# A planned kernel on one core: products of ones, split halves, one more vt load, joined additions, and a new order of all steps

## The chip, the cores and the metric
One core of a Trainium2 chip. The metric is device microseconds of one execution, as the median of three. Times inside an execution come from one profiled execution and count from its first instruction.

## The reference
q, k and v are float32 of shape (4, 5056, 256), normal values times 0.1. Per batch:
```python
qn = q / (norm(q, axis=1) + 1e-6);  kn = k / (norm(k, axis=1) + 1e-6)
s = kn.T @ qn / tau                      # 256 x 256
a = softmax(s, axis=-1)
x = v @ a                                # 5056 x 256
```
Then a soft mixture of 8 experts with 4 slots each over all 20224 rows x: `logits = x @ phi` (32 columns); softmax over the rows gives the slots' inputs `d.T @ x`; each expert computes `relu(in @ w1) @ w2` (256 to 1024 to 256); softmax over the 32 columns weights the slots' outputs into the result (20224 x 256).

## The kernel before
Five engines and one DMA queue (SP's) work through one list of steps. A program of `at(...)` calls puts some thousand steps into `plan`; ORDER, a list of numbers worked out beforehand, says in which order they are called (lines 1037 to 1039). Each engine takes its own steps in that order, and so does SP's queue. A step whose inputs are not there holds up all that stand behind it on its engine.

- SBUF has 22 big buffers of 1 MB. HOME says which buffer a tile takes; the tile waits until all readers of the buffer's tile before it are done.
- q and k come in 40 units u (4 batches, 10 units each; batches share units 9 and 29, called MIX): tile raw{u}, up to four row blocks j of 128 rows. `load_qk` (line 141) loads unit 0 in two parts, and all others in one.
- `score(u, j, split)` (line 237) adds a row block into k.T @ q. Plain, it multiplies the float32 tile (two products, each of which the trace shows as two matmuls). For the halves (u, k) in SPLIT, `cast` (ScalarE) and `low` (VectorE, line 209) first make a high and a low part in a tile hl{u}_{k}, and score makes three products of each of the two column halves: six matmuls for a row block.
- `square` (ScalarE) and `add` (VectorE, lines 232 to 235) sum the squares of the columns, for the norms. Before, the additions of units 11 to 38 come as two instructions of 1024 columns, those of units 1 to 9 as one of 2048.
- v comes in 20 tiles p of eight row blocks. x = v @ a is never formed: v's transpose (tile x{p}) is multiplied with the small matrix M = a @ phi (`logits`, line 393). Each half m of that transpose is loaded from a copy in memory (`load_vt`, line 156) if (p, m) is in LT; otherwise TensorE turns it (`turn`, line 373: four transposes for each half h) and ScalarE evicts it (`turned`).
- `gather` (line 495) sums the slots' inputs; the steps join_ and last_ put them together; `up`, `relu`, `flip_h`, `back_h`, `down` (lines 671 to 717) are the experts. `down(r, h, f)` makes the column half h and needs w2 tiles of that half. `o_copy`, `o_fold`, `o_back` finish a half; then `out_mul` (line 740) and `out_evict` make the result of a row tile, `store` writes it. Ten stores of batch 0 go by column halves, the first half's before the second half's downs are done.
- `c_max` to `c_flip` are the softmax over the columns, on VectorE and ScalarE.
- `wake` (line 784) multiplies ones with ones on TensorE, at the very start.

Of the kernel before, what the change touches and what calls it, by code (L numbers as in the profile page):

```python
# [20 lines left out]
WAKE = 9  # L21
PITCH = 128
NU = B * UB
NRAW = 5
MIX = (UB - 1, 3 * UB - 1)
SPLIT = {(u, 0) for u in range(1, NU) if u not in (1, 2, 3, 17, 20, 27, 31)} | {(u, 1) for u in (2, 5, 14, 24, 26, 27, 31, 33, 35, 37, 39)}
LT = {(p, 0) for p in (0, 2, 3, 4, 5, 6, 7, 8, 9, 11, 12, 13, 15, 18, 19)} | {(p, 1) for p in (0, 3, 6, 9, 12, 15)}
GR = {b: (3, 2) for b in range(B)}
HOME = {
    "raw0": 0, "raw1": 1, "raw2": 2, "raw3": 3, "raw4": 4, "sq0": 5, "sq1": 6, "sq2": 8, "hl2_1": 7, "sq3": 18,  # L30
    "hl4_0": 19, "sq4": 20, "v1": 8, "raw5": 9, "raw6": 10, "raw9": 11, "raw8": 12, "raw7": 13, "v4": 7, "hl5_0":
    21, "sq5": 6, "hl6_0": 1, "x1": 20, "hl5_1": 0, "hl9_0": 2, "sq6": 3, "sq9": 7, "sq10": 6, "hl8_0": 8, "hl7_0":
    18, "raw13": 17, "sq8": 20, "sq7": 4, "raw12": 0, "raw10": 16, "x0": 18, "raw16": 19, "raw17": 14, "hl13_0": 4,
    "sq13": 10, "hl10_0": 7, "hl12_0": 17, "x4": 0, "sq12": 16, "raw14": 13, "v2": 14, "raw18": 12, "hl14_1": 14,
    "hl14_0": 4, "sq17": 3, "hl16_0": 18, "sq14": 10, "hl18_0": 11, "v5": 19, "raw19": 15, "raw11": 21, "raw15": 1,
    "v7": 13, "sq16": 16, "sq19": 20, "hl19_0": 9, "hl15_0": 13, "hl11_0": 16, "sq15": 0, "raw20": 2, "raw21": 15,
    "x2": 21, "raw24": 19, "sq18": 1, "sq11": 3, "hl24_1": 6, "sq20": 1, "sq21": 12, "hl21_0": 10, "hl24_0": 3,
    "sq24": 15, "raw23": 5, "raw25": 4, "v0": 2, "raw22": 9, "raw28": 11, "x5": 8, "raw29": 17, "hl23_0": 10,
    "sq23": 20, "hl25_0": 21, "sq22": 12, "sq25": 3, "hl28_0": 10, "hl22_0": 18, "raw26": 16, "x3": 5, "raw27": 20,
    "raw31": 11, "sq28": 9, "sq29": 6, "sq30": 14, "hl29_0": 18, "hl26_0": 5, "hl27_1": 16, "sq26": 10, "x7": 6,  # L40
    "sq27": 21, "raw30": 15, "v3": 9, "v8": 21, "raw32": 3, "hl26_1": 15, "hl31_1": 18, "sq31": 1, "hl32_0": 20,
    "sq32": 5, "hl30_0": 2, "x6": 10, "v11": 15, "raw33": 12, "raw34": 0, "raw37": 1, "raw38": 17, "hl33_1": 2,
    "sq33": 15, "hl34_0": 10, "hl33_0": 8, "x8": 11, "sq37": 2, "sq34": 16, "hl37_1": 9, "raw39": 4, "v6": 12,
    "v10": 7, "x9": 9, "x12": 1, "x11": 13, "raw36": 5, "raw35": 3, "hl38_0": 6, "sq39": 20, "hl37_0": 18, "sq38":
    12, "hl39_1": 12, "sq36": 19, "x10": 10, "sq35": 8, "v13": 2, "v17": 20, "v9": 0, "v14": 16, "v19": 11,
    "hl35_1": 21, "hl35_0": 10, "hl36_0": 11, "x13": 6, "hl39_0": 19, "x14": 0, "x15": 8, "x18": 13, "v18": 5,
    "v16": 17, "v12": 18, "w1_0": 15, "x19": 12, "x17": 10, "x16": 3, "nat0": 1, "v15": 19, "w1_1": 4, "w1_7": 7,
    "w1_3": 6, "w1_4": 14, "w1_6": 9, "w1_2": 21, "w1_5": 18, "nat3": 12, "w2_1_0": 3, "w2_0_0": 0, "w2_2_0": 8,
    "w2_3_0": 10, "w2_1_1": 16, "w2_0_1": 2, "w2_2_1": 1, "w2_3_1": 13, "nat2": 19, "hs0": 17, "hT0": 20, "hs1": 5,
    "hT1": 11, "o0_1": 15, "o0_2": 4, "o0_0": 21, "o0_4": 6, "o0_3": 17, "o3_3": 14, "o3_1": 9, "o2_1": 18, "nat1":  # L50
    7, "o2_2": 5, "o3_2": 0, "o2_0": 8, "o3_4": 3, "o2_4": 2, "o3_0": 10, "o1_2": 16, "o1_3": 20, "o1_4": 1, "o1_0":
    11, "o1_1": 13, "o2_3": 12,
# [3 lines left out]
    1, 7, 14, 18, 0, 2, 3, 5, 4, 9, 12, 11, 20, 10, 21, 28, 6, 13, 38, 29, 634, 22, 113, 135, 49, 76, 8, 15, 23, 30,  # L56
    34, 39, 43, 50, 47, 77, 26, 27, 36, 37, 25, 17, 16, 19, 24, 31, 35, 44, 40, 51, 48, 78, 54, 81, 68, 59, 63, 72,
    174, 55, 69, 60, 83, 175, 64, 73, 531, 532, 32, 57, 56, 33, 46, 42, 45, 53, 52, 75, 84, 74, 65, 66, 79, 80, 71,
    61, 41, 181, 92, 159, 161, 121, 177, 91, 156, 87, 114, 178, 118, 70, 176, 182, 122, 533, 85, 103, 67, 93, 123,
    86, 145, 58, 601, 163, 155, 173, 88, 115, 119, 534, 82, 535, 111, 117, 62, 89, 116, 143, 162, 112, 160, 144,  # L60
    154, 108, 104, 164, 146, 124, 128, 120, 109, 536, 110, 538, 165, 147, 158, 157, 105, 129, 125, 537, 132, 530,
    150, 98, 140, 136, 171, 153, 172, 185, 186, 131, 107, 90, 539, 130, 391, 387, 149, 148, 126, 127, 167, 166, 198,
    187, 102, 197, 106, 133, 134, 179, 152, 540, 151, 137, 141, 180, 543, 183, 607, 602, 600, 189, 219, 599, 231,
    190, 94, 168, 392, 541, 388, 544, 194, 191, 142, 95, 170, 546, 169, 99, 100, 551, 552, 193, 545, 389, 192, 139,
    542, 397, 138, 97, 96, 390, 228, 547, 398, 184, 548, 385, 399, 101, 188, 386, 549, 220, 210, 400, 608, 614, 199,
    603, 598, 553, 437, 440, 393, 272, 217, 218, 271, 282, 196, 195, 554, 211, 221, 212, 213, 223, 222, 395, 208,
    555, 224, 438, 200, 214, 441, 550, 394, 204, 264, 229, 556, 230, 215, 225, 216, 558, 439, 201, 265, 557, 236,
    396, 239, 226, 443, 559, 266, 407, 207, 240, 227, 267, 203, 206, 205, 445, 237, 238, 442, 560, 446, 606, 605,
    241, 609, 209, 444, 232, 268, 447, 278, 250, 233, 269, 448, 449, 280, 454, 563, 281, 270, 251, 273, 263, 253,
    333, 615, 604, 202, 235, 401, 234, 450, 453, 463, 467, 455, 274, 561, 564, 258, 242, 285, 402, 289, 451, 408,  # L70
    275, 259, 252, 286, 260, 571, 452, 572, 284, 612, 610, 613, 616, 283, 290, 262, 261, 300, 276, 288, 277, 287,
    403, 299, 573, 246, 456, 292, 316, 468, 247, 457, 574, 566, 243, 458, 293, 405, 249, 562, 565, 309, 245, 244,
    248, 575, 279, 296, 459, 567, 460, 254, 485, 461, 297, 298, 317, 568, 306, 569, 404, 320, 472, 481, 464, 469,
    323, 617, 311, 620, 621, 576, 462, 255, 482, 466, 312, 324, 406, 465, 302, 411, 318, 257, 483, 409, 256, 473,
    310, 295, 319, 294, 307, 471, 322, 308, 313, 475, 484, 578, 325, 321, 303, 476, 470, 328, 365, 362, 410, 412,
    474, 570, 477, 354, 486, 332, 331, 304, 327, 417, 326, 305, 619, 301, 611, 622, 291, 618, 329, 363, 487, 479,
    355, 577, 418, 382, 493, 488, 491, 501, 505, 579, 315, 372, 357, 314, 423, 421, 358, 489, 345, 349, 369, 424,
    422, 342, 364, 383, 330, 490, 580, 492, 359, 495, 384, 366, 370, 583, 346, 350, 496, 353, 373, 413, 419, 360,
    356, 361, 348, 368, 581, 494, 506, 420, 414, 497, 584, 582, 415, 585, 352, 347, 416, 587, 627, 629, 626, 637,
    623, 625, 633, 624, 755, 638, 640, 371, 499, 343, 351, 586, 588, 427, 431, 367, 589, 498, 378, 374, 478, 428,  # L80
    502, 510, 519, 507, 435, 344, 590, 375, 504, 591, 520, 379, 334, 338, 503, 436, 432, 592, 511, 335, 593, 639,
    628, 631, 750, 753, 632, 594, 433, 521, 429, 509, 513, 522, 595, 430, 512, 508, 434, 381, 336, 337, 524, 656,
    650, 673, 523, 597, 339, 525, 480, 500, 765, 766, 514, 651, 657, 596, 380, 340, 654, 425, 341, 377, 376, 655,
    515, 426, 636, 648, 652, 635, 517, 767, 667, 670, 649, 653, 768, 668, 671, 526, 529, 666, 674, 669, 672, 528,
    675, 677, 681, 769, 678, 642, 646, 679, 676, 643, 647, 680, 644, 527, 516, 645, 683, 702, 692, 664, 662, 686,
    689, 770, 518, 771, 709, 832, 684, 688, 694, 835, 691, 712, 665, 663, 703, 658, 660, 704, 705, 751, 630, 641,
    752, 756, 749, 757, 754, 763, 761, 759, 758, 659, 661, 687, 682, 690, 714, 716, 695, 760, 833, 834, 685, 706,
    698, 717, 831, 697, 715, 713, 693, 718, 764, 762, 699, 707, 721, 722, 719, 701, 708, 724, 720, 723, 700, 696,
    726, 728, 731, 725, 733, 710, 786, 732, 727, 729, 734, 730, 740, 741, 735, 736, 711, 737, 742, 738, 743, 745,
# [14 lines left out]
def colnorm_attention_soft_moe(  # L104
# [59 lines left out]
    def load_few():  # L164
        sp.dma_start(few_sb, few)

    load_qk(0, ((0, 1), (1, 4)))
    for u in range(1, NRAW):
        load_qk(u)

# [621 lines left out]
    def at(key, f, *a):  # L792
        plan.append((key, len(plan), f, a))

    at(-2, wake, WAKE)
    FV = 13
# [299 lines left out]
```

## Time and profile before

| | us |
|---|---|
| median of 3 runs | 277.02 (276.91 to 278.49) |
| profiled execution | 277.06 |
| its span, first to last instruction | 275.3 |
| TensorE busy | 254.6 (92%) |
| VectorE busy | 236.8 (86%) |
| ScalarE busy | 195.5 (71%) |
| moved by DMA | 111.44 MB, 405 GB/s over the span |

The span is shorter than the time by 1.76 us, which lie outside the recorded instructions. Matmuls overlap, so TensorE's busy time is the time in which at least one was under way. The DMA share is the mean busy share of the 16 DMA engines; it can come out slightly over 1. "Landing" of a DMA is the time from its issue by SP to its completion.

### The profile page before, as it was taken

Reading aid. Unit: us, or ns where it says so; the run is one execution under the profiler, and the core shown is the slowest. Engines: PE = TensorE matmul, PEld = TensorE weight load, DVE = VectorE, ACT = ScalarE, POOL = GpSimd, SP = SyncE. Lnnn points to the kernel's source line nnn. Section 1 sums busy time; section 2 is a strip of 40 time slices with the busy share of each in tenths; the row PEclk is TensorE's granted clock in tenths of the full one; section 3 lists DMA queues with packets and bytes.
Section 4 is the critical chain, followed back from the end, with each engine's and each line's share of the span. In section 5 each row is a group of like instructions: output and inputs, shape, how many; then the busy total and the mean of one; then the engine's idle time right before and its main releaser. Section 6 shows DMA issues by size and latency. Waiting matters only on the chain.

```text
span 275.3 us, 6127 instructions
## 1 busy us (share of the span) xinstructions
PE 254.6 (92%) x2494; PEld 212.6 (77%) x2494; DVE 236.8 (86%) x349; ACT 195.5 (71%) x285; POOL 7.5 (3%) x12
## 2 busy tenths in 40 slices
PE   8999999999999999999999999999999988678730
PEld 8889998999998896997898978866555878457520
DVE  1599999999999999999999997887989879988630
ACT  3898989798899689899998783886416247353430
POOL 1000002000002000020000001000000000000000
PEclk9999999999999999999999999999999999855755
DMA  7999999999999999999999999999999789999995
GB/s 283 432 424 410 422 426 415 420 417 419 419 417 420 412 422 421 416 415 417 412 419 418 416 417 419 417 416 420 421 415 420 300 332 388 418 418 412 420 421 246
DMA packets 17883, 111.44 MB, mean 405 GB/s; under 512 B 2112, under 2 KB 2112, under 8 KB 6592
## 3 DMA queue, kind: packets, MB, share of 16 engines
q1 hardware_dynamic: 17856, 111.06, 98.0%
q8 instruction: 19, 0.31, 0.4%
q14 instruction: 8, 0.07, 0.1%
HBM read 90.08 MB, written 20.97 MB: 403 GB/s over the span
## 4 chain that ended last, share of the span: by engine, by line
PE 87%; DVE 6%; ACT 3%; issue 1%; DVEq 0%; ACTq 0%
PE S L255 46%; PE op_None L750 8%; PE L L403 7%; PE G L503 7%; PE vTp L376 6%; PE op L750 3%; PE O L711 2%; DVE o L774 2%; ACT o L772 2%; PE wake L787 2%; PE Mp L347 1%; PE nn L266 1%; DVE nat L630 1%; DVE cm L627 1%; PE sp L549 1%; PE gt L525 1%
## 5 line engine op out<-in xcount | busy, mean ns | idle before, releaser
L235 DVE TENSOR_TENSOR sq<-sq,sq 128x1024 f32<-128x1024 f32 (+1 forms) x61 | 81.3, 1356 | 8.4 <-ACT sq L220 8.0
L220 ACT ACTIVATE sq<-raw 128x2048 f32<-128x2048 f32 (+1 forms) x40 | 74.7, 1889 | 6.5 <-DMA raw<-in_qk_dram 4.8
L255 PE MATMUL S<-hl 128*128 128x256 f32 x516 | 71.5, 291 | 0.0
L255 PE MATMUL S<-raw 128*128 128x256 f32 (+1 forms) x296 | 66.9, 384 | 0.0
L255 PEld LDWEIGHTS S<-hl 128*128 128x128 f32 x516 | 65.2, 191 | 1.0
L255 PEld LDWEIGHTS S<-raw 128*128 128x128 f32 (+1 forms) x296 | 53.7, 192 | 8.1 <-issue 1.5
L209 DVE TENSOR_TENSOR hl<-raw,hl 128x1024 fp32r<-128x1024 f32 x43 | 51.6, 1219 | 0.7 <-ACT hl L204 0.7
L204 ACT CAST hl<-raw 128x1024 fp32r<-128x1024 f32 x43 | 44.0, 1048 | 6.1 <-PE S L255 2.5
L750 PE MATMUL op_None<-so,lg 32*128 32x256 f32 x240 | 26.4, 525 | 6.0 <-ACT o L772 4.1
L772 ACT COPY o<-op_None 128x512 f32<-128x512 f32 x30 | 15.8, 594 | 18.2 <-PE op_None L750 17.9
L750 PEld LDWEIGHTS op_None<-so,lg 32*128 32x128 f32 x240 | 19.6, 251 | 11.6 <-ACT o L772 6.3
L381 ACT COPY x<-vTp 128x512 f32<-128x512 f32 x38 | 21.5, 593 | 9.3 <-PE vTp L376 8.8
L774 DVE COPY o<-op_None 128x512 f32<-128x512 f32 x30 | 19.0, 678 | 8.0 <-PE op_None L750 8.0
L376 PE MATMUL vTp<-ident,v 128*128 128x128 f32 x152 | 21.6, 276 | 0.0
L403 PE MATMUL L<-x,M 128*32 128x256 f32 (+1 forms) x320 | 20.3, 379 | 0.0
L376 PEld LDWEIGHTS vTp<-ident,v 128*128 128x128 f32 x152 | 17.3, 143 | 2.8 <-issue 2.5
L503 PE MATMUL G<-v,dn 128*32 128x256 f32 x320 | 19.1, 381 | 0.0
L503 PEld LDWEIGHTS G<-v,dn 128*32 128x32 f32 x320 | 10.8, 110 | 5.9 <-issue 0.7
L403 PEld LDWEIGHTS L<-x,M 128*32 128x32 f32 x320 | 9.8, 109 | 6.2 <-issue 0.8
L750 PE MATMUL op<-so,lg 32*128 32x128 f32 x160 | 9.6, 315 | 2.0 <-ACT o L772 1.4
L750 PEld LDWEIGHTS op<-so,lg 32*128 32x128 f32 x160 | 7.7, 197 | 4.4 <-ACT o L772 2.7
L772 ACT COPY o<-op 128x256 f32<-128x256 f32 x20 | 6.4, 378 | 6.3 <-PE op L750 6.3
(112 smaller groups left out, 233.0 us busy)
## 6 DMA issues: line engine op xcount, KB each, us to landing
raw<-in_qk_dram SPq DMA_DIRECT2D x37, 1024.0 KB, 12.5
v<-in_v_dram SPq DMA_DIRECT2D x20, 1024.0 KB, 11.1
w<-in_moe_w_dram SPq DMA_DIRECT2D x16, 1024.0 KB, 17.5
out_dram<-o SPq DMA_DIRECT2D x15, 1024.0 KB, 7.5
x<-in_vt_dram SPq DMA_DIRECT2D x17, 512.0 KB, 10.2
out_dram<-o SPq DMA_DIRECT2D x10, 512.0 KB, 3.7
raw<-in_qk_dram SPq DMA_DIRECT2D x3, 768.0 KB, 10.0
x<-in_vt_dram SPq DMA_DIRECT2D x4, 480.0 KB, 11.9
```

What stands on the lines that cost most here:

```text
L204: act.copy(hl[:, :, 0::2, :], raws[u][:, 2 * k : 2 * k + 2])
L209: dve.tensor_tensor(hl[:, :, 1::2, :], raws[u][:, 2 * k : 2 * k + 2], hl[:, :, 0::2, :].bitcast(F32), op=ALU.subtract)
L220: act.activation(sq_tile(u)[:, :n], raws[u][:, :n], AF.Square)
L235: dve.tensor_tensor(a[:, lo:hi], a[:, lo:hi], s[:, lo:hi], op=ALU.add)
L255: pe.matmul(sm, w, x, start=first[bb], stop=False, skip_group_check=True)
L376: pe.transpose(tp[:, P * jj : P * jj + P], vs[p][:, 4 * h + jj, P * m : P * m + P], ident)
L381: act.copy(x[:, h * UT : h * UT + UT], tps[p, h, m])
L403: pe.matmul(L[S * g : S * g + S, :n, :], M[:, m, :], x[:, :n, S * g : S * g + S], start=m == 0, stop=m == 1,)
L503: pe.matmul(gp[S * g : S * g + S, :C], dn[:, x, j, :], vt[:, j, :], start=x == 0 and j < G, stop=x == n - 1 and j >= G,)
L750: pe.matmul(ops[b, p, hf, g][:, h, :], cT[b][S * g : S * g + S, 4 * i : 4 * i + 4, :].rearrange("s j t -> s (j t)"), so[S * g : S * g + S] ...
L772: act.copy(dst, src)
L774: dve.tensor_copy(dst, src)
```

## The change
- WAKE: six products of ones instead of nine.
- Unit 0 is loaded as row blocks 0 and 1, then 2 and 3 (512 KB each), instead of 0, then 1 to 3.
- SPLIT: 40 halves instead of 43. (5,0), (5,1), (7,0), (13,0), (19,0), (27,1), (32,0), (37,0), (39,0) become plain; (8,1), (11,1), (13,1), (23,1), (27,0), (34,1) become split.
- LT: (14, 0) is added. One vt load of 512 KB more, two turns (and evictions) fewer: 957 steps in place of 992, with the additions.
- `add`: one instruction of 2048 columns for units 11 to 38 too (26 pairs); unit 39 keeps two.
- HOME and ORDER are new throughout.

```diff
-WAKE = 9
+WAKE = 6
...
-SPLIT = {(u, 0) for u in range(1, NU) if u not in (1, 2, 3, 17, 20, 27, 31)} | {(u, 1) for u in (2, 5, 14, 24, 26, 27, 31, 33, 35, 37, 39)}
-LT = {(p, 0) for p in (0, 2, 3, 4, 5, 6, 7, 8, 9, 11, 12, 13, 15, 18, 19)} | {(p, 1) for p in (0, 3, 6, 9, 12, 15)}
+SPLIT = {(u, 0) for u in range(1, NU) if u not in (1, 2, 3, 5, 7, 13, 17, 19, 20, 31, 32, 37, 39)} | {(u, 1) for u in (2, 8, 11, 13, 14, 23, 24, 26, 31, 33, 34, 35, 37, 39)}
+LT = {(p, 0) for p in (0, 2, 3, 4, 5, 6, 7, 8, 9, 11, 12, 13, 14, 15, 18, 19)} | {(p, 1) for p in (0, 3, 6, 9, 12, 15)}
...
+    1, "x10": 13, "v11": 4, "raw36": 7, "raw35": 9, "v13": 15, "x12": 6, "v17": 1, "v9": 19, "v14": 11, "hl38_0":
+    20, "sq38": 16, "sq36": 10, "x11": 21, "hl35_1": 18, "sq35": 0, "hl35_0": 16, "hl36_0": 3, "x13": 5, "hl39_1":
+    12, "x14": 20, "v12": 10, "v16": 0, "w2_0_0": 7, "x15": 2, "v18": 19, "w1_6": 13, "w1_7": 8, "v19": 9, "x17":
...
-    load_qk(0, ((0, 1), (1, 4)))
+    load_qk(0, ((0, 2), (2, 4)))
...
         if i:
-            if u > 9:
-                at(u + (0.55 if u < NU - 1 else 0.05), add, u, 0, 2)
-                at(u + (0.72 if u < NU - 1 else 0.06), add, u, 2, 4)
+            if u == NU - 1:
+                at(u + 0.05, add, u, 0, 2)
+                at(u + 0.06, add, u, 2, 4)
             else:
                 at(u + 0.60, add, u, 0, 4)
```
ORDER, read as steps, where the text below needs it (f(u, ...) as in the code; the last argument of score is split):
```
TensorE, start, new: wake; score (0,0) (0,2) (0,1) (0,3) (1,1) (1,0) (1,2) (2,1) (2,0) (1,3) (3,2) (3,0) (3,3) (3,1) (4,2) (5,0) (5,3) (4,3) (6,2) (6,3), all plain
SP, new:            ... load_v(9) load_v(14) load_vt(12,1) load_vt(14,0) load_vt(11,0) load_vt(13,0) load_v(12) load_v(16) load_w2(0,0) ...
TensorE, new:       ... turn(13,1,1) turn(10,0,1) score(38,0,1) att_phi(2) gather(8) gather(9) logits(10) turn(14,1,1) ...
TensorE, before:    ... att_phi(2) turn(13,1,1) turn(14,0,1) score(38,0,1) logits(10) gather(8) gather(9) ...
TensorE, before:    ... down(1,0,*) down(0,1,0) o_fold(0) down(0,1,6) out_mul down(0,1,2) out_mul down(0,1,4) out_mul out_mul down(1,1,*) out_mul o_fold(1) ...
TensorE, new:       ... down(1,0,*) o_fold(0) down(0,1,0) out_mul down(0,1,4) out_mul down(0,1,2) out_mul down(0,1,6) out_mul down(1,1,*) out_mul o_fold(1) ...
SP, last loads:     before w2 (0,1) (1,1) (3,1) (2,1); new w2 (0,1) (1,1) (2,1) (3,1)
ScalarE:            before relu(0,0) relu(0,1) c_exp(3) relu(1,1) c_exp(2) back_h(0,1) relu(1,0); new relu(0,1) relu(0,0) c_exp(3) c_exp(2) relu(1,1) relu(1,0) back_h(0,1)
```

## Rows read from the trace of the kernel before
**Rows 1.** The page: span, and the granted TensorE clock in 40 slices.
```profile
span 275.3 us, 6127 instructions
PEclk9999999999999999999999999999999999855755
```
**Rows 2.** Stages: start:end, length; busy us (xinstructions) of each engine, clock, DMA share, GB/s.
```profile
0.00:158.00 158.00, 156.96 (x1212) 141.46 (x1212) 146.75 (x175) 138.59 (x152) 6.47 (x11) 1.00 1.00 413
12.00:165.00 153.00, 153.00 (x1260) 136.69 (x1258) 150.52 (x177) 137.30 (x158) 5.77 (x5) 1.00 1.02 418
165.00:200.00 35.00, 35.00 (x434) 25.43 (x433) 28.59 (x78) 21.64 (x61) 1.01 (x1) 1.00 1.02 417
200.00:217.40 17.40, 16.93 (x265) 10.69 (x261) 16.45 (x24) 6.49 (x10) 0.00 (x0) 1.00 0.99 411
217.40:229.00 11.60, 10.71 (x253) 8.88 (x253) 8.72 (x22) 5.56 (x19) 0.00 (x0) 1.00 0.74 295
229.00:272.40 43.40, 28.03 (x255) 20.91 (x251) 29.56 (x44) 17.77 (x35) 0.00 (x0) 0.65 1.01 415
```
**Rows 3.** The chain of waits in order of time: start us, us, what, instructions.
```profile
73.33 1.43 PE S L255 x12
79.29 1.73 PE S L255 x8
148.53 0.87 PE vTp L376 x8
158.08 0.81 PE Mp L347 x8
159.80 0.71 PE S L255 x6
216.86 0.57 PE O L711 x16
222.41 1.89 PE O L711 x64
224.29 0.73 PE op L750 x16
```
**Rows 4.** Groups by form, VectorE and ScalarE: busy us, mean ns of one, idle before.
```profile
L235 DVE TENSOR_TENSOR sq<-sq,sq 128x1024 f32<-128x1024 f32 x53 | 63.0, 1215 | 0.4 <-ACT sq L220 0.2
L209 DVE TENSOR_TENSOR hl<-raw,hl 128x1024 fp32r<-128x1024 f32 x43 | 51.6, 1219 | 0.7 <-ACT hl L204 0.7
L204 ACT CAST hl<-raw 128x1024 fp32r<-128x1024 f32 x43 | 44.0, 1048 | 6.1 <-PE S L255 2.5 <-DMA raw<-in_qk_dram 2.5 <-DVE sq L235 0.6
L235 DVE TENSOR_TENSOR sq<-sq,sq 128x2048 f32<-128x2048 f32 x8 | 18.3, 2289 | 8.0 <-ACT sq L220 7.8
```
**Rows 5.** Timeline of the start: start us, us, engine, line, operation, idle before.
```profile
0.73 5.17 SPq L146 DMA_DIRECT2D raw<-in_qk_dram  x10
1.04 4.21 PE L787 MATMUL wake<-ones 128*128 128x128 f32 x18 [1.04 <-DVE half L176]
4.84 11.24 PEld L255 LDWEIGHTS S<-raw 128*128 128x128 f32 x49
5.65 1.91 ACT L220 ACTIVATE sq<-raw 128x2048 f32<-128x2048 f32 x1 [3.43 <-DMA raw<-in_qk_dram]
...
5.05 14.67 PE L255 MATMUL S<-raw 128*128 128x256 f32 x64
```
**Rows 6.** DMA from 0 to 16 us in 40 bins; an issue, its us to landing.
```profile
GB/s 0 0 0 0 128 195 364 353 384 399 445 446 481 369 389 492 430 328 492 471 348 471 451 389 430 451 430 348 512 451 328 471 471 369 430 492 389 389 430 492
raw<-in_qk_dram SPq DMA_DIRECT2D x1, 256.0 KB, 2.6
```
**Rows 7.** Timeline of SP's queue: issues of loads, start us, us.
```profile
157.40 1.04 SPq L154 DMA_DIRECT2D v<-in_v_dram  x2
...
195.40 5.29 SPq L666 DMA_DIRECT2D w<-in_moe_w_dram  x3
```
**Rows 8.** Issues and us to landing: the second of those at 157.4, the last w.
```profile
v<-in_v_dram SPq DMA_DIRECT2D x1, 1024.0 KB, 16.0
w<-in_moe_w_dram SPq DMA_DIRECT2D x1, 1024.0 KB, 19.9
```

## What the change will do, predicted before it ran
> **What bounds the kernel now.** The table by stage comes first [rows 2]: from 12 to 165 us TensorE is busy in all of the 153 us and the DMA engines are full (share 1.02, 418 GB/s); so it stays to 200 us. Two resources are at their limit together. From 200 to 217.4 us TensorE still works 16.93 of 17.40 us (the expert stage) and the queue still carries loads. Only from 217.4 to 229 us does the DMA drop, to 295 GB/s: the loads have ended and the outputs are not yet there in number. From 229 to 272.4 us stores run at 415 GB/s, and the kernel ends with them; the clock that TensorE has lost by then [rows 1] costs nothing. So the end is set by (a) when out_mul for the two halves of batch 0 can start and (b) the bytes that are left then. (a) hangs on TensorE's total work and on the landing of the last w2 tiles, which stand at the end of one SP queue: the last three were issued in 5.29 us from 195.4 on, the last of them near 200.4 [rows 7], and took 19.9 us to land [rows 8], so 220.3 us.
>
> How much the DMA can give at all: the dip costs 11.6 us x (1 - 295/418) = 3.4 us. Closing all of it, with 1.26 us of new bytes (below), would bring 2.1 us, 0.8%.
>
> **TensorE's work.** In the chain of waits, in order of time, twelve split products (two tiles) take 1.43 us and eight plain ones (two tiles) 1.73 us [rows 3]. A half unit therefore costs 0.30 us more plain than split. Splits fall from 43 to 40 halves: +0.90 us. Two turns fewer at 0.87/2 us: -0.87 us. Sum +0.03 us, nothing. All else on TensorE is the same set of steps in another order.
>
> **VectorE and ScalarE.** Three casts at 1.05 us (-3.1 us) and two evictions of turns leave ScalarE. Three subtractions at 1.22 us leave VectorE, and 26 pairs of additions become one: 2 x 1.215 - 2.289 = 0.14 us each, 3.7 us [rows 4]. These 7.4 us lie beside a full TensorE [rows 2], and after 200 us VectorE's steps are the same ones, so I cost them at zero; if TensorE were waiting for VectorE, the relief would be worth up to that much. It isn't: TensorE shows no idle there. GpSimd's few steps keep their places among the norms and lie beside the same work. The Trainium skill (VectorE: DVE Perf Modes, section "The TRN2 errata") says that every SBUF-source instruction pays a fixed extra, about 150 cycles of 0.96 GHz; by it, as an estimate, a pair joined saves 0.16 us and all 26 save 4.1 us. The rows say nearly the same, and the sum is the same by both, since none of it is on the path.
>
> **The start.** Nine products of ones are 18 instructions in 4.21 us, 0.234 us each; then S begins at 5.05 us (its weights at 4.84) [rows 5]. Six end at 1.04 + 12 x 0.234 = 3.85 us. The first part of unit 0 is now 512 KB instead of 256. The old 256 KB took 2.6 us from its issue at 0.73, so 3.3 us; adding up the GB/s bins of 0.4 us, 0.262 MB had moved by 2.76 us and 0.524 MB by 3.5 us [rows 6], so the new part lands some 0.6 us behind that, at 4.1 us. S can start 0.8 us sooner. It doesn't keep all of it: 64 products from 5.05 us on took 14.67 us [rows 5] against 64 x 0.216 = 13.8, so some three of them ran at half rate. The records show a granted clock of full speed (2.4 GHz) in this stretch [rows 1], which does not fit; I go by the durations. Begun sooner, two or more in addition run at half rate. Gain 0.4 us, bounds 0 and 0.8. And the data are now close: unit 0 is complete at 5.65 us [rows 5], each further unit 1.049 MB / 0.418 = 2.5 us later, so unit 5 at 18.2 and unit 6 at 20.7. In the new order fifteen plain tiles (0.865 us) stand before unit 5's first: 4.1 + 13.0 + 1.1 (slow ones) = 18.2 us; unit 6 comes three tiles later, 20.8 us. No slack is left, where the old order had one to two us.
>
> **One more load, and where it stands.** vt(14,0) is 0.524 MB: 1.26 us at 418 GB/s, and every load behind it lands so much later. What matters more is its buffer. In HOME, x14 takes number 20 after hl38_0. Its last reader is score(38,0,1) on TensorE, and SP issues in order, so this load and all behind it (vt(11,0), vt(13,0), v12, v16, all w) wait for that step.
> - When is it free? Before, these six products end at 159.80 + 0.71 = 160.5 us [rows 3]. In the new order there stand ahead of them 6 split tiles fewer (-4.3), 5 plain ones more (+4.3), one turn fewer (-0.44) and att_phi(2) no longer (-0.81): -1.2 us. With the 0.4 us of the start: 158.9 us.
> - When is the queue empty? Ahead of it stand all 40 q/k units (38 of 1.049 MB and 2 of three quarters, 41.4 MB), 15 v (15.7), 15 vt (7.8): 64.95 MB. By 158.0 us the engines had moved 158.0 x 413 = 65.25 MB [rows 2], some 0.3 MB of it instructions. They run dry at 157.9 us.
> - The first load of the kernel is issued at 0.73 us [rows 5] and bytes appear in the bin from 1.6 us [rows 6]: 0.9 us. Data flow again from 158.9 + 0.1 + 0.9 = 159.9 us.
>
> So the full queue gets a hole of some 2.0 us, between 0 (if TensorE is 2 us sooner than I add up) and 3.5. The kernel before has none like it: at 158 us a load had 16.0 us from issue to landing [rows 7, 8]. I take 2.0, since both ends come from sums over rows of the same stage.
>
> **The end.** Without the hole the last loads land 1.26 us later than before, with it 3.3 us. The last three w2 were issued 2.5 us apart and, at 19.9 us each, landed at 215.3, 217.8 and 220.3 [rows 7, 8]; they come to 218.6, 221.1 and 223.6. Now o_fold(0) stands before down(0,1,0), and the first out_mul behind that. down(0,1,0) needs the third last w2: 218.6 us; sixteen products of a down take 0.57 us [rows 3], so out_mul begins at 219.2 instead of 216.86 + 0.57 = 217.4, +1.8. Four out_mul of 0.73 us and three downs of 0.57 later, at 223.8, come the four downs that need the last w2 (223.6); before they began at 222.4 [rows 3]. +1.4 us. From there the second half's stores run as before, at full rate. The moved relu(1,1), now behind both c_exp, costs 0.1 us, hidden under the wait for w2. Span 275.3 + 1.4 = 276.7; the profiled execution took 277.06, 1.76 more than its span, and lies 0.04 us over the median of 277.02, so 278.4. Since the hole's bounds lie more below than above, I put it at 278.2 us.
>
> **Rivals.**
> 1. No hole. TensorE reaches score(38,0,1) by 156.9, or the 16 DMA engines run dry so unevenly that the hole fills. Then 218.6 becomes 216.6, where TensorE arrives anyway; the four downs start at 221.8, 0.5 us sooner than before: 276.5 us. For it: the sum leaves only 2 us. Against it: the plan puts this load behind that step whatever the rest does.
> 2. Slower by over 1%. TensorE waits for data in the first 45 us, at units 5 and 6 and those close behind, where the new order has no slack. TensorE being full after that, each us of wait comes to score(38,0,1) a us late, and the hole widens by as much, while the DMA runs dry at the same time as ever. From 1.4 us of such waits on (hole 3.4 us) the result is +2.8 us, 279.8. Two us of waits: 280.4. For it: slack of zero; against it: the waits end once TensorE is behind.
> 3. The clock. Half rate lasts past unit 0: 13 more products at 0.216 us extra are 2.8 us, which go into the hole as above: +4.2, 281.2 us. Against it: the engine is kept at work from 1.04 us almost without a gap. The Trainium skill (TensorE: Matmul & The Clock Gate, section "Loop structure matters more than you think") says that waiting for DMA between matmuls lets the array fall to half clock; fewer products of ones and a later first part go that way. No trace here shows it yet.
> 4. Faster by over 1%. It needs more than the whole dip; only if transfers ran faster.
>
> **How the numbers follow.** Forecast (hole of 1 to 3.3 us) 0.50; rival 1 0.28; rival 2 0.16; rival 3 0.03; rival 4 0.02; anything else slow 0.01. A measurement here can tell about 1% (2.8 us). Faster 0.02; within 1%, 0.50 + 0.28 = 0.78; slower 0.20. The range from 276.2 (rival 1 with all 0.8 us of the start) to 280.2 leaves about 2 in 10 outside; the forecast's own is 277.3 to 279.7.
>
> **What will show it.** The DMA row of the changed kernel has a notch at 157 to 160 us, and SP's issue of a vt load comes near 159 us with PE S L255 as its releaser. TensorE has a wait of one to two us on a w load near 217 us. The first out_mul begins at 219, the second half's fold is later by about 1.4 us. S begins near 4.1 us. Wrong it would be if the row stays at 418 through 160 us, if out_mul begins at or before 217.4, or if TensorE idles between 45 and 150 us for VectorE or ScalarE, for which I see no cause.

## The result, and the profile after

The changed kernel takes 280.06 us (median of six, 279.75 to 281.43). The kernel before, with three more runs beside it, stands at 278.12 (six, 276.91 to 278.49). The ratio is 1.0101, interval 1.0079 to 1.0123: about 1% slower. It is not the quotient of the two medians (1.007): both kernels' times stand in two groups some 1.3 us apart, the medians fall into different ones, and like with like the ratio is 1.011 in the lower group (276.97 and 279.92 us) and in the upper (278.26 and 281.34). The profiled executions have spans of 278.1 and 275.3 us, +2.8. The forecast was 278.2, no change that could be told; the time lies near the top of its range, in the place of rival 2.

| | before | after |
|---|---|---|
| span | 275.3 | 278.1 |
| VectorE / ScalarE busy, us | 236.8 / 195.5 | 232.6 / 191.7 |
| moved by DMA, MB | 111.44 | 111.93 |
| TensorE ends score(38,0,1) | 160.5 | 160.0 |
| first out_mul / last four downs begin | 217.4 / 222.3 | 220.8 / 225.2 |

Lines of the code stand two lower than before (score is L253, add L233, out_mul L748, down L709). In runs 6, 7 and 8 they stand one lower than before. The stages of after, columns as in [rows 2], where their counterparts are:
```profile
12.00:45.00 33.00, 32.47 (x188) 28.81 (x188) 30.89 (x22) 27.79 (x22) 0.52 (x1) 1.00 1.02 421
...
157.00:165.00 8.00, 8.00 (x97) 6.69 (x95) 8.00 (x8) 5.34 (x12) 0.00 (x0) 1.00 0.62 213
165.00:200.00 35.00, 34.93 (x432) 25.71 (x435) 26.70 (x73) 20.29 (x58) 1.01 (x1) 1.00 1.02 420
...
217.40:229.00 11.60, 9.76 (x248) 7.32 (x240) 8.68 (x18) 3.67 (x12) 0.00 (x0) 1.00 0.96 387
```
One stage is new: from 157 to 165 us the DMA moved 213 GB/s where before it was full:
```profile
157.00:165.00 8.00, 8.00 (x104) 6.22 (x102) 7.75 (x11) 5.82 (x12) 0.00 (x0) 1.00 1.03 421
```
Against 418 GB/s that is 8 x (1 - 213/418) = 3.9 us of transfer lost. The dip from 217.4 to 229 us is nearly gone (387 against 295 GB/s), but only because loads now reach into it. These two and the added bytes make up the result: 3.9 us lost in the hole, 1.2 us for the 0.49 MB more, and (387 - 295)/418 x 11.6 = 2.6 us less lost in the dip, +2.5 us in all, where +2.8 were measured. The same balance comes within 0.6 us of the ratio of every run below but the fifth, where the stage of the stores was slower too. It says where the time lies, not why. The granted clock is 1.00 in every row: rival 3 did not happen.

The hole in bins of 0.4 us, from 152 to 168 us of after:
```profile
GB/s 451 410 348 512 389 389 430 430 420 358 440 430 266 236 236 236 82 31 20 31 0 0 96 115 211 326 348 329 377 410 430 399 410 440 492 389 410 451 451 410
```
The rate halves at 156.8 us, is nearly zero from 158.4 to 160.8, and climbs for 2.4 us before it is full again. The ramp costs 1.0 us (the six bins from 160.8 to 163.2 against 418).

SP's queue (timeline: start us, us), and its wait by the list of waits (us in total, times, longest):
```profile
147.59 0.42 SPq L158 DMA_DIRECT2D x<-in_vt_dram  x1
...
160.06 0.33 SPq L160 DMA_DIRECT2D x<-in_vt_dram  x1
160.44 0.90 SPq L158 DMA_DIRECT2D x<-in_vt_dram  x2
```
```profile
SPq L160 <- PE S L253: 7.7, 2, 5.6
```
L160 is the load of vt(14,0), released by PE S L253, a score. On TensorE that score and what came after it, in the order of the chain and then of the timeline of its end (start us, us):
```profile
159.28 0.71 PE S L253 x6
...
199.87 20.31 DMA w<-in_moe_w_dram
220.22 0.63 PE O L709 x12
```
```profile
220.22 0.63 PE L709 MATMUL O<-w,hT 128*32 128x128 f32 x12 [0.91 <-DMA w<-in_moe_w_dram]
220.78 0.73 PE L748 MATMUL op<-so,lg 32*128 32x128 f32 x16
...
225.18 1.95 PE L709 MATMUL O<-w,hT 128*32 128x128 f32 x64
```
score(38,0,1) ends at 159.99 and 0.07 us later the load is issued. At the other end a w2 that was issued at 199.87 lands at 220.2, TensorE waits for it, and the first out_mul begins at 220.78 [rows 3 had the downs that need the last w2 at 222.41; here they begin at 225.18].

### The profile page after: what moved, and what is told of

Its sections match the earlier page's. It is cut to its first block, busy times and chain, and to the rows that moved or that the text cites. A ratio compares the mean times of both kernels' runs of the same rounds, so it can differ in the third digit from the quotient of the medians.

```text
span 278.1 us, 6035 instructions
## 1 busy us (share of the span) xinstructions
PE 252.2 (91%) x2468; PEld 209.3 (75%) x2468; DVE 232.6 (84%) x320; ACT 191.7 (69%) x280; POOL 9.6 (3%) x12
## 2 busy tenths in 40 slices
DMA packets 18027, 111.93 MB, mean 402 GB/s; under 512 B 2128, under 2 KB 2128, under 8 KB 6736
## 4 chain that ended last, share of the span: by engine, by line
PE 63%; DMA 24%; DVE 5%; ACT 3%; issue 1%; SPq 0%; ACTq 0%
PE S L253 36%; DMA w<-in_moe_w_dram 14%; DMA raw<-in_qk_dram 11%; PE vTp L374 5%; PE L L401 5%; PE op_None L748 5%; PE G L501 4%; ACT o L770 3%; PE op L748 2%; DVE o L772 2%; PE O L709 2%; PE nn L264 1%; PE Mp L345 1%; PE rq L296 1%; PE aTp L333 1%
## 5 line engine op out<-in xcount | busy, mean ns | idle before, releaser
L233 DVE TENSOR_TENSOR sq<-sq,sq 128x2048 f32<-128x2048 f32 (+1 forms) x35 | 77.8, 2224 | 10.3 <-ACT sq L218 9.9
L253 PE MATMUL S<-raw 128*128 128x256 f32 (+1 forms) x320 | 73.6, 386 | 0.9 <-DMA raw<-in_qk_dram 0.9
L253 PE MATMUL S<-hl 128*128 128x256 f32 x480 | 67.3, 292 | 0.0
L253 PEld LDWEIGHTS S<-raw 128*128 128x128 f32 (+1 forms) x320 | 58.1, 193 | 9.7 <-DMA raw<-in_qk_dram 1.9
L253 PEld LDWEIGHTS S<-hl 128*128 128x128 f32 x480 | 60.9, 191 | 1.0
L207 DVE TENSOR_TENSOR hl<-raw,hl 128x1024 fp32r<-128x1024 f32 x40 | 47.8, 1215 | 0.1
L202 ACT CAST hl<-raw 128x1024 fp32r<-128x1024 f32 x40 | 40.6, 1045 | 3.4 <-DMA raw<-in_qk_dram 1.8
L748 PE MATMUL op_None<-so,lg 32*128 32x256 f32 x240 | 24.6, 492 | 9.7 <-ACT o L770 4.0
L748 PEld LDWEIGHTS op_None<-so,lg 32*128 32x128 f32 x240 | 18.0, 237 | 15.4 <-ACT o L770 6.8
L420 ACT COPY lg<-L 128x256 f32<-128x256 f32 x20 | 7.4, 376 | 7.2 <-DVE mxs L430 4.7
L274 POOL TENSOR_TENSOR rn<-rn,half 128x4 f32<-128x4 f32 x4 | 7.9, 1964 | 104.2 <-DVE rn L269 104.2
```

The lines of the kernel that those rows point to most:

```text
L202: act.copy(hl[:, :, 0::2, :], raws[u][:, 2 * k : 2 * k + 2])
L207: dve.tensor_tensor(hl[:, :, 1::2, :], raws[u][:, 2 * k : 2 * k + 2], hl[:, :, 0::2, :].bitcast(F32), op=ALU.subtract)
L233: dve.tensor_tensor(a[:, lo:hi], a[:, lo:hi], s[:, lo:hi], op=ALU.add)
L253: pe.matmul(sm, w, x, start=first[bb], stop=False, skip_group_check=True)
L748: pe.matmul(ops[b, p, hf, g][:, h, :], cT[b][S * g : S * g + S, 4 * i : 4 * i + 4, :].rearrange("s j t -> s (j t)"), so[S * g : S * g + S] ...
```

## The experiments

Edits are given as moves in the order of steps; ratios are to the kernel before, run on the same chip.

**1. The load out of the way.** Only the place in SP's queue changes.
```
-SP: ... load_vt(12,1) load_vt(14,0) load_vt(11,0) load_vt(13,0) load_v(12) load_v(16) ...
+SP: ... load_vt(12,1) load_vt(11,0) load_vt(13,0) load_v(12) load_v(16) load_vt(14,0) ...
```


> The changed kernel with one load moved: vt(14,0) stands behind v16 in SP's queue, not ahead of vt(11,0). All else is the same, so its buffer is still free only after score(38,0,1), but four loads go out before that. Theory (the hole of 3.9 us at 157 to 162 us costs the time): the DMA row stays at about 418 GB/s through 157 to 165 us, the first out_mul starts near 217.2 instead of 220.85, the four last downs near 222 instead of 225.2; 2.8 us less than the changed kernel, so 0 to 0.5 us less than before. Rival (the new order elsewhere, or the 0.5 MB more, costs it): the hole goes and the time stays within 1 us of the changed kernel, 1.5 to 2.8 us above before.

277.95 us, ratio 1.0021 (1.0002 to 1.0040), span 275.6. Its row for the stage, and its first out_mul and last downs:
```profile
157.00:165.00 8.00, 8.00 (x97) 6.69 (x95) 7.99 (x8) 5.34 (x12) 0.00 (x0) 1.00 1.02 414
```
```profile
218.00 0.73 PE L748 MATMUL op<-so,lg 32*128 32x128 f32 x16
...
222.59 1.95 PE L709 MATMUL O<-w,hT 128*32 128x128 f32 x64
```
The same bytes, the same buffer, that one load still issued at 160.01 us, and no hole: the ratio falls by 0.8%, 2.2 us (I had expected 2.8). The wait costs only through what stands behind it in the queue.

**2 and 3. The size of the hole.** Here the load keeps its place, and TensorE frees its buffer sooner: both readers of hl38_0 move ahead.
```
-TensorE: ... score(38,3,0) score(36,2,0) score(34,0,1) score(38,1,1) turn turn score(38,0,1) ...
+e5:      ... score(38,3,0) score(36,2,0) score(38,1,1) score(38,0,1) score(34,0,1) turn turn ...
+e6:      ... score(38,1,1) score(38,0,1) score(38,3,0) score(36,2,0) score(34,0,1) turn turn ...
```


> The changed kernel with score(38,1,1) and score(38,0,1), the two readers of the buffer that vt(14,0) waits for, moved on TensorE ahead of score(34,0,1) and two turns; nothing else moves. By the sum of the trace the buffer is free at 158.4 us instead of 160.0. Theory A (the wait for this buffer makes the hole; its size is the time of the issue less a fixed point): the issue comes at 158.5, the hole shrinks from 3.9 to 2.3 us, the first out_mul begins near 219.2 to 219.5 (220.8 with the change, 218.0 without the hole), ratio to before 1.005 to 1.007. Rival B (the hole comes from loads and buffers behind it, this wait is only the first of them): the hole stays near 3.9 us, ratio 1.009 to 1.011.

> The same two scores moved further ahead, in front of score(38,3,0) too: the buffer is free near 156.7 us, when the DMA of the changed kernel just begins to run dry (156.8). Theory A: issue at 156.8, hole of 0 to 0.7 us, first out_mul 218.0 to 218.3, ratio 1.002 to 1.003 as with the load moved behind load_v(16). Rival B: hole near 3.9 us still, ratio 1.009 to 1.011. If the hole goes faster than the wait (a fixed part of it is lost as soon as the queue does not run dry), e5 and e6 show it: 3.9 us for an issue at 160.06, x for 158.5, y for 156.8 lie on a line of slope 1 or do not.

The moderate move gave 279.38 us, ratio 1.0051 (1.0031 to 1.0071), span 276.2; the far one 277.95, ratio 1.0022 (0.9997 to 1.0047), span 275.4. The spans and rows are those of one execution each, of 277.94 and 277.19 us, the first of them the fastest of its twelve. The load's issue and the stage, moderate move first:
```profile
158.35 0.33 SPq L160 DMA_DIRECT2D x<-in_vt_dram  x1
```
```profile
157.00:165.00 8.00, 8.00 (x97) 6.67 (x95) 7.98 (x8) 5.33 (x12) 0.00 (x0) 1.00 0.86 322
```
```profile
156.60 0.33 SPq L160 DMA_DIRECT2D x<-in_vt_dram  x1
```
```profile
157.00:165.00 8.00, 8.00 (x92) 6.52 (x90) 7.99 (x8) 5.33 (x12) 0.00 (x0) 1.00 1.00 388
```
Worked out as above, issues at 156.60, 158.35 and 160.06 us lose 0.6, 1.8 and 3.9 us. The hole is the time of the issue less some 156.2 us, to within 0.4 us: on the whole microsecond for microsecond, as theory A had it, with no lump that falls away at once. The first out_mul follows: 217.86, 218.82 and 220.78 us. Rival B, other buffers behind this one, is out.

**4. The start alone**, in the old kernel: WAKE = 6, and unit 0 in row blocks (0, 2), (2, 4).

> The kernel before with the start alone: six products of ones, and unit 0 in two parts of 512 KB. Theory: S starts 0.7 us sooner, some of it lost to products at half rate, and the end comes 0 to 0.5 us sooner. Rival (the clock rises later with fewer products of ones, and TensorE loses by it): 0.5 to 2 us later.

277.26 us, ratio 0.9999 (0.9980 to 1.0019). TensorE's timeline of this kernel, and of before:
```profile
4.33 15.45 PE L255 MATMUL S<-raw 128*128 128x256 f32 x64 [0.36 <-DMA raw<-in_qk_dram]
19.43 2.50 PE L255 MATMUL S<-hl 128*128 128x256 f32 x18
```
```profile
5.05 14.67 PE L255 MATMUL S<-raw 128*128 128x256 f32 x64
19.37 2.50 PE L255 MATMUL S<-hl 128*128 128x256 f32 x18
```
The products begin 0.72 us sooner and take 0.78 us longer; the next step begins at the same time. One pair of traces can't show what the start is worth, since six kernels with the same start (before, and runs 5, 6, 7, 10, 11) differ as much: 14.36 to 15.08 us, the next step at 19.05 to 19.78. What differs is when the clock rises. The trace's list of clock records begins with a record of full clock at 6.45 us in the kernel before and at 7.14 in this one; for the stretch ahead of it there is no record, and the views print 1.00 there. So the 1.00 that did not fit the durations in the prediction was no record. The products' durations show it (ns, lowest/median/highest, first and last start in us), here of before, of this kernel, and of the far move of run 3, whose first record is at 4.07:
```profile
L255 PE MATMUL S<-raw x3: 634/634/634, 5.0 to 5.9; 128*128 128x256 f32 x3
```
```profile
L255 PE MATMUL S<-raw x7: 424/634/795, 4.3 to 7.1; 128*128 128x256 f32 x7
```
```profile
L253 PE MATMUL S<-raw x11: 379/379/483, 4.3 to 7.0; 128*128 128x256 f32 x11
```
In the times themselves, the start alone brings nothing that ten executions can tell; the interval leaves room for 0.5 us.

**5. A hole in the old kernel.** load_w1(2), whose buffer is free late, ahead of five loads it stood behind. The expectation calls this the only edit; load_vt(13,0) and load_vt(18,0) change places too.
```
-SP: ... load_vt(18,0) load_vt(13,0) load_vt(15,0) load_w1(1) load_w1(4) load_vt(15,1) load_w1(2) ...
+SP: ... load_vt(13,0) load_w1(2) load_vt(18,0) load_vt(15,0) load_w1(1) load_w1(4) load_vt(15,1) ...
```


> The kernel before with one thing done to it: w1(2), whose buffer comes free with score(35,3,1) near 175 us, is put ahead of vt(18,0), vt(15,0), w1(1), w1(4) and vt(15,1) in SP's queue. No work is added. The queue runs dry near 173.4 us by the bytes ahead, so a hole of some 3.4 us. Theory: the last w2 land 3.4 us later, out_mul starts near 219.8 instead of 217.4 at the earliest, and the time rises by 2.3 to 3.0 us. Rival (a hole is absorbed by the dip at 217 to 229 us): under 1 us.

282.81 us, ratio 1.0176 (1.0142 to 1.0210), span 281.1: nearly twice the price expected. TensorE's wait and the matmuls of up(), the stages, and the clock in two parts of them, of this kernel, then up() of before:
```profile
189.96 2.68 PE L403 MATMUL L<-x,M 128*32 128x256 f32 x24 [2.31 <-DMA x<-in_vt_dram]
...
206.94 7.05 PE L677 MATMUL H<-w,slT 128*32 128x512 f32 x48
```
```profile
165.00:200.00 35.00, 32.69 (x380) 23.97 (x383) 25.26 (x67) 20.55 (x56) 1.01 (x1) 0.95 0.92 376
200.00:217.40 17.40, 17.11 (x176) 8.51 (x171) 15.02 (x28) 6.56 (x14) 0.00 (x0) 0.90 1.01 420
```
```profile
190.00:193.50 3.50, 3.50 (x29) 1.92 (x30) 1.86 (x7) 0.00 (x0) 0.00 (x0) 0.52 1.04 428
...
207.20:210.60 3.40, 3.40 (x20) 0.87 (x16) 3.40 (x3) 0.21 (x2) 0.00 (x0) 0.50 1.02 417
```
```profile
202.67 5.36 PE L677 MATMUL H<-w,slT 128*32 128x512 f32 x48
```
The hole is as large as expected: (417 - 376)/418 x 35 = 3.4 us. But it reached TensorE itself, which waited 2.3 us for a vt that was late. Right behind that wait the granted clock fell to 0.5 (1.2 GHz). The Trainium skill (TensorE: Matmul & The Clock Gate, section "Loop structure matters more than you think") says that a long wait for DMA between matmuls lets the array fall to half clock; this trace agrees, with 0.52 in the row from 190.0 us. A second stretch at 0.50 lies in up(), whose 48 products took 7.05 us, where before they took 5.36. No wait for data stands ahead of that one, so its cause stays open. The first out_mul came at 223.07 us, 5.7 later than before: the 2.3 us of waiting, 1.7 us in up(), and 1.7 us, by estimate, for the first stretch at half clock. So this hole was not absorbed, and one that starves TensorE can cost more than its own length. In the changed kernel the late loads were not needed soon, and its clock stayed at 1.00 until 242 us.

**6 and 7. The joined additions**, in the old kernel: all 26 pairs, then only those of units 11 to 35.
```
-add(u,0,2) ... add(u,2,4)
+               add(u,0,4)
```


> The kernel before with the joined additions alone: 26 pairs become one instruction each at the place of the second. Theory: VectorE is busy 3.7 us less and the time stays within 0.5 us, as TensorE is full beside it. Rival (VectorE is the bound between 14 and 165 us): 2 to 4 us less.

> The kernel before with the additions joined for units 11 to 35 only (22 or so pairs; 36, 37 and 38 stay pairs). With all joined it was 0.3% slower, and its TensorE fell back 0.41 us in the first matmuls, where no addition stands, and 0.65 us at 164.5 to 168 us, at nn of the last batch and gt, behind two joined additions of 2.25 us on VectorE. Theory: it is the last three alone that cost; ratio 0.999 to 1.0015, nn of the last batch within 0.2 us of its old time, VectorE still some 3 us less busy. Rival: an addition of 2048 columns holds up what stands behind it wherever it is: ratio 1.003 again, with TensorE idle in several places.

278.24 us, ratio 1.0030 (1.0012 to 1.0048), and 278.20, ratio 1.0031 (1.0010 to 1.0052): slower by 0.8 us, where the theory for all joined had 0.5 at most, and the theory that the last three units alone cost is wrong. VectorE and TensorE with all joined, then TensorE with units 11 to 35 joined, then two additions of before:
```profile
159.47 2.27 DVE L234 TENSOR_TENSOR sq<-sq,sq 128x2048 f32<-128x2048 f32 x1
...
161.78 1.22 DVE L259 TENSOR_TENSOR sq<-sq 128x1024 f32<-128x1024 f32 x1
```
```profile
165.13 1.05 PE L265 MATMUL nn<-ones,sq 128*128 128x1 f32 x8
```
```profile
157.12 0.44 PE L334 MATMUL aTp<-ident,a 128*128 128x128 f32 x2 [0.37 <-ACT a L317]
```
```profile
46.56 2.35 DVE L235 TENSOR_TENSOR sq<-sq,sq 128x1024 f32<-128x1024 f32 x2
```
With all joined the last sum of the norms begins at 161.78 (160.24 before), and TensorE's nn at 165.13 instead of 164.52; 0.4 us of these 0.6 were there at 20 us already, where the clock rose later (the 64 products of the start took 15.08 us). With part of them joined the wait stands at aTp, behind the softmax. These waits fit the loss, but no run took one of them away. Busy time of VectorE fell by 1.5 us only (236.8 to 235.3), not by the 3.7 of the prediction.

**8. Pairs again**, in the new order without its hole (the far move of run 3).

> The changed kernel without its hole (the two scores ahead), with the additions of units 11 to 38 in two instructions again, at the place of the one. In the kernel before, joining them cost 0.3% through short steps of the softmax and the norms that stood behind an addition of 2.25 us on VectorE (aTp waited 0.37 us for ScalarE, nn 0.2, gt 0.35). Theory: the new order was laid for the joined form, TensorE shows no such wait in it, so pairs bring nothing: ratio to before 1.001 to 1.004, as with joined ones (1.0022). Rival: the joined form costs here as well: pairs bring 0.3%, ratio 0.998 to 1.000.

278.60 us, ratio 1.0050 (1.0030 to 1.0070), no better than joined (1.0022); the intervals overlap. TensorE's timeline has a wait that the joined form had not:
```profile
80.35 1.02 PE L265 MATMUL nn<-ones,sq 128*128 128x1 f32 x8 [0.36 <-DVE sq L259]
```
By this wait the load of vt(14,0) came later too, at 157.31 us instead of 156.60, and its stage lost 0.9 us instead of 0.6. That each order favours the form that it was laid out for is how I read runs 6 to 8; it isn't shown. In the changed kernel the joined additions are not what made it slower.

**9. Without the added load.** (14,0) is turned on TensorE as before; LT without (14, 0), all else as changed but for two evictions of ScalarE, of x17, that move ahead.

> The changed kernel without its added load: (14,0) is turned on TensorE and evicted by ScalarE as before; start, splits, joined additions and order stay. Theory A: no wait, no hole; TensorE 0.87 us later in the expert stage than in the kernel with the load moved (first out_mul 218.8 to 219.0), 1.26 us of bytes fewer: ratio 0.999 to 1.003. Rival C (the new start, the splits and the joined additions cost the greater part, the load is harmless): ratio 1.007 or more.

279.02 us, ratio 1.0057 (1.0038 to 1.0075), span 277.3: 1.2 us better than the change by the ratios, 1 us worse than keeping the load in a better place, where I had expected a small gain. The dip of this kernel, then of the one with the load moved:
```profile
217.40:229.00 11.60, 10.37 (x248) 7.88 (x244) 8.91 (x18) 3.97 (x14) 0.00 (x0) 1.00 0.60 237
```
```profile
217.40:229.00 11.60, 11.08 (x278) 9.08 (x279) 9.99 (x22) 5.58 (x19) 0.00 (x0) 1.00 0.80 318
```
The first out_mul came at 218.89, as expected, 0.9 us later than with the load moved. The dip got wider at both ends: the loads end 1.2 us sooner by the bytes, and the first results come 0.9 us later. It lost (318 - 237)/418 x 11.6 = 2.2 us more, and the 1.2 us of bytes saved is less than that. So the load itself was a good trade; its place was not.

**10 to 12. A kernel that beats both?** Up to here each span ended 52.8 to 53.3 us after the last four downs began. If that rule were a cause, downs that begin sooner would bring the end forward.
```
-TensorE (before): ... out_mul(0,0) out_mul(0,4) down(1,1,*) out_mul(0,3) o_fold(1) ...
+e9:               ... out_mul(0,0) down(1,1,*) out_mul(0,4) o_fold(1) out_mul(0,3) ...
+e10:              ... down(1,1,*) out_mul(0,0) o_fold(1) out_mul(0,4) out_mul(0,3) ...
```


> The kernel before with one out_mul of the first column half, (0,4), moved on TensorE from ahead of the last four downs to behind them, and the one that stood there, (0,3), moved behind o_fold(1), where TensorE waits 0.52 us for ScalarE; their evictions and stores follow. In all kernels so far the span ends 52.8 to 53.3 us after the last four downs begin. Rule 1 (the end is set by when the second half comes): the downs begin 0.66 us sooner, at 221.7 (the last w2 landed at 220.3), span 274.6 to 274.9, ratio 0.997 to 0.9985. Rival (the end is set by when the first stores keep the queue busy, the 53 us only go with it): two stores of the first half come 2.5 us later, so no gain or a loss, ratio 1.000 to 1.004.

> As in the run with one moved, but two: out_mul (0,0) and (0,4) stand behind the last four downs, (0,0) at once, (0,4) behind o_fold(1), (0,3) behind that. The downs begin 1.3 us sooner (221.0), but the first out_mul of the second half only some 0.6 us sooner, since the two fill more than the 0.52 us that TensorE waited. By last downs + 53: span 274.0, ratio 0.995 to 0.997. By the second half's first out_mul: 0.6 us, ratio 0.998. By the supply of the first stores: ratio 1.000 to 1.006.

> The changed kernel without its hole (the two scores ahead, buffer free at 156.7), with down(0,1,0) ahead of o_fold(0) as in the kernel before (0.41 us of waiting for VectorE gone), and with the move of one out_mul as above. The sum says 1.07 us sooner than that kernel without the last two edits; but its last w2 is issued at 201.98 and lands near 221.8, 0.65 us before its downs began (222.45). Theory: the downs begin at 221.8, the gain is 0.5 to 0.7 us, ratio to before 0.999 to 1.001. If the end hangs on the first stores: 1.001 to 1.004.

277.57 us, ratio 1.0005 (0.9985 to 1.0025); 277.63, ratio 1.0000 (0.9982 to 1.0019); and 278.67, ratio 1.0052 (1.0030 to 1.0075). The downs with one and with two moved, and the dip of the latter:
```profile
221.30 1.96 PE L711 MATMUL O<-w,hT 128*32 128x128 f32 x64
```
```profile
219.94 2.69 PE L711 MATMUL O<-w,hT 128*32 128x128 f32 x80
```
```profile
217.40:229.00 11.60, 10.75 (x252) 8.69 (x241) 8.27 (x21) 5.02 (x17) 0.00 (x0) 1.00 0.68 277
```
With two moved the row's 80 products hold the 16 of down(0,1,4), which now stands just ahead; by where the rows end, the last four downs came 1.0 and 1.7 us sooner. The spans were 275.4 and 275.9 us, no shorter than the 275.3 of before, so that they end 54.1 and some 55.2 us after those downs begin. The rule fell: the downs had only gone along. With two moved the dip lost (295 - 277)/418 x 11.6 = 0.5 us more and the profiled span grew by 0.6; over all executions the ratio shows no change. The third, which puts this move on the new order, lost too; its first out_mul waited 0.35 us for ScalarE where the fold now stood close ahead of it. None beats the kernel before.

## Why the prediction was right or wrong

**Where it goes: right.** The stall of vt(14,0), its releaser, the empty DMA near 158 to 160 us, the late w2, TensorE's wait for it and the late out_mul all came as told, and taking the load out of the way took 2.2 us back.

**The step that failed is the sum for the hole**, 2.0 us where 3.9 were measured. Two of its terms were mis-sized.
- "158.9 us" for the free buffer was 160.0. The sum gave the start a gain of 0.4 us and let TensorE be full from there on. In the trace TensorE is idle 0.53 us ahead of 31.88 us, waiting for raw16 (by the count of products). Here are the changed kernel, then the moderate and the far move of runs 2 and 3:
```profile
31.88 1.99 PE L253 MATMUL S<-raw 128*128 128x256 f32 x8 [0.53 <-DMA raw<-in_qk_dram]
```
```profile
31.76 1.99 PE L253 MATMUL S<-raw 128*128 128x256 f32 x8 [0.23 <-DMA raw<-in_qk_dram]
```
```profile
31.73 1.99 PE L253 MATMUL S<-raw 128*128 128x256 f32 x8 [0.54 <-DMA raw<-in_qk_dram]
```
  All seven kernels with the new order go on between 31.69 and 32.00 us, though their first 80 products end anywhere from 22.61 to 23.34. So it is the queue that sets the time there, and whatever the start gains is waited away. My estimate found no slack at units 5 and 6 but was not carried on to the units behind them. The gain of 0.4 and the wait of 0.53 are 0.9 of the 1.1 us. Rival 2 named this mechanism; its waits were below the 1.4 us I asked for, and the result came out in its place only because the next term went the same way.
- "Dry at 157.9, data again 0.9 us after the issue" took the DMA as a switch. Both figures were right: the bins up to 160.8 us lose as much as an end at 157.9 would, and the first bytes come between 160.8 and 161.2, about 0.9 us after the issue. But the rate was full only 2.2 us after that, which cost some 0.8 to 1.0 us more, and the sum had no term for it.

The load is also a little smaller than the sum had it: the bytes rose by 0.49 MB and not 0.524, 1.2 us at 418 GB/s and not 1.26.

**From the hole to the end: right in form.** The sum had a w2 at 218.6, out_mul at 219.2 and the last downs at 223.8, with 2.0 us of hole. They came at 220.2, 220.8 and 225.2, each 1.4 to 1.6 us later, for 1.9 us more hole, and the span grew by the same 1.4 us over what I had added up.

**TensorE's work: right.** Without the hole (run 1) TensorE begins up() at 203.33 us, 0.66 later than the 202.67 of before. The work was to add 0.03 us; in this trace TensorE waits 0.8 us for raw between 26 and 32 us and 0.15 us at zp. The parts were not taken away one by one.

**VectorE at zero: right for this kernel, for a poorer reason than I gave.** The saving was 1.5 us and not 3.7, since additions that stand back to back overlap: two of 1.22 us took 2.35 us together, one joined 2.28, a gain of 0.07 us a pair. By the Trainium skill (VectorE: DVE Perf Modes, section "The TRN2 errata") the estimate was 4.1 us; the rows of these runs do not bear that out for neighbouring instructions. And going by TensorE's lack of idle missed that a longer instruction delays short ones behind it, on which TensorE waits: runs 6 and 7 lost 0.3%.

**How much the DMA can give: not to be had that way.** I priced the dip at 3.4 us. The changed kernel closed 2.6 us of it and the moderate move 2.0, but with loads that came late: hole and added bytes cost more, 5.1 and 3.0 us. Fewer bytes ahead of it (run 9) and out_mul put off (runs 10 and 11) widened it.

The chances put 0.28 on no hole and 0.20 on slower by over 1%. Since slack of zero at the start, a gain there that is waited away and a gradual refill all push one way, the bounds of the hole (0 to 3.5 us) should have reached above 4.

What stays open: why the kernel without its hole is still 0.2% above the one before, if it is (the far move's interval reaches down to 0.9997). By the balance of run 1, 1.2 us of added bytes less (318 - 295)/418 x 11.6 = 0.6 us that the dip gave back are the 0.6 us; no run tests that.

## What to carry to other kernels

When a load is moved or added in an in-order queue, find the last reader of its buffer and ask when the queue ahead of it is empty; if the two times are close, the price is what stands behind it, so put such a load behind those whose buffers are free. Price the hole with its ramp, and let every uncertain term that delays the reader widen it. A gain ahead of a wait for data is worth nothing, so follow the queue's landing times up to the last unit that is multiplied as soon as it lands. A regularity over many traces (here the end 53 us after the downs) is a cause only once it has been pushed.

## What the runs showed of the hardware

- A dry queue takes time to fill: after the issue at 160.06 us the first bytes came between 160.8 and 161.2 and the full rate at 163.2.
- The hole that one late load made in the queue was its issue less some 156.2 us: issues at 156.60, 158.35 and 160.06 us lost 0.6, 1.8 and 3.9 us of transfer.
- TensorE multiplied ones from 1.04 us on in every kernel, and its clock rose between 4.07 and 7.28 us, with nine such products or six: a product's instruction took 634 ns ahead of that and 379 behind. The first 64 float32 products took 14.36 to 15.08 us in six kernels with the same start. The list of clock records begins only with the rise, and the 1.00 that views print ahead of it is no record.
- After 2.3 us of waiting for data the granted clock fell to 0.5, and once more at 207.2 us, in up(), where 48 matmuls took 7.05 us instead of 5.36.
- Two back-to-back additions of 128x1024 took 2.35 us, one of 128x2048 took 2.28 us, though each short one is listed with 1.22.
